# A ring of four places for streamed weights instead of six, with 15 instead of 17 streamed units

## The chip, the cores and the metric

The kernel runs on one core of a Trainium2 chip. The metric is the device time of one execution in microseconds, lower is better. Three runs of the kernel before took 1783.06, 1787.77 and 1794.25 us; the median is 1787.77 us. One more number is used throughout: the profiled execution, whose rows are quoted, spans 1793.2 us from its first to its last instruction.

PE stands for TensorE, DVE for VectorE, ACT for ScalarE, POOL for GpSimd and SP for SyncE, which only issues transfers here. PEld is TensorE's weight load. A name with a q, such as SPq, is an engine's sequencer.

## The reference

```python
xn = layernorm(x)                          # x: 2048 tokens of 1024, bfloat16
out = x + A(xn) + B(xn)

def B(xn):                                 # w1: 1024 x 3584, w2: 3584 x 1024
    return gelu(xn @ w1 + b1) @ w2 + b2

def A(xn):                                 # 32 heads of 128; Wq, Wk, Wv: 1024 x 4096, Wo: 4096 x 1024
    mem = mem0                             # 8 rows of 1024
    for s in range(64):                    # segments of 32 tokens
        h = concat(mem, xn[32 * s: 32 * s + 32])       # 40 rows
        q, k, v = h @ Wq, h @ Wk, h @ Wv
        p = softmax(mask(q @ k.T / sqrt(128)))         # per head; memory columns are always seen
        o = (p @ v) @ Wo
        mem = o[:8]                        # carried into the next segment
        outs.append(o[8:])
    return concat(outs)
```

The memory rows that leave segment s enter segment s + 1, so the 64 segments run one after the other. Each of them multiplies 40 rows by all four weight matrices, 33.5 MB in bfloat16, which is more than the on-chip memory holds.

## The kernel before

**Two stages.** The first 440 us compute B for all tokens (with the layer norm), and keep x + B as rows in DRAM. The rest is the recurrence of A over 64 segments. In its products the 24 rows of a segment's first tokens and the 8 memory rows are the stationary operand (32 columns), and the weights stream past them as the moving operand. Four matmuls run side by side on four groups of 32 PE columns, so one product of 32 rows with a unit of weights is four matmuls of 128x512 (L830). The last 8 tokens of each segment, which nothing later depends on, are gathered over four segments into 32 "left" rows and multiplied once per group of four. Which left products fall into a segment makes four kinds of segment, `i4 = s % 4`: kind 0 has those of K1 and V0, kind 1 of Q0 and of O, kind 2 of Q1, kind 3 of K0 and V1.

**Units and passes.** The weights are 64 units of 128 partitions x 2048 values (512 KB, 4 KB in each partition). A segment goes through them in a fixed order: eight units each for the half passes K0, Q0, K1, Q1, V0, V1 and then sixteen for O. A unit is named by matrix, row and half; `Wc_K_3_0` is K's row block 3 in half 0. `half_pass` runs the first six groups, the loop over `O_UNITS` the last sixteen; `at` lists give what is done behind the n-th unit of a pass, such as the scores of heads (`scores`, L947 and L953), their sums (`sums`, L985 and L991), and `values` (L1039 and L1045).

**Resident and streamed units.** 47 of 64 units stay on chip during the recurrence (`RESIDENT`, each in a place named in `RES_PLACES`, which the first stage used before for other data). 17 are streamed: needed once per segment, fetched anew each time. `PLACED` has, for each kind of segment, one string per group of eight units, where an S stands for a streamed unit and a point for a resident one; inside a group of eight the order of the units is free, so the S's can be moved. `kind_order` turns it into the order of a segment.

Two of the 17 are not fetched from DRAM. `IN_PSUM`, the fourth streamed unit (in Q0), and `IN_BANKS`, the last one (in O), are kept in four PSUM banks and copied by DVE into the ring, two copies of 128x512 32-bit words each (`copy_bits`, L273). The other 15 come as one transfer each from contiguous copies `Wc_...` in DRAM, which the first stage made.

**The ring.** Streamed units pass through the places in `RING`. When the last product with a streamed unit is issued, `unit_done` calls `start_stream` with the place that comes free, and this starts the next streamed unit in the order `starts`: a transfer on SP's queue (L284) that waits for PE's last matmul on the old unit, or the DVE copies, which wait for the same. With six places a unit begins six streamed uses ahead of its own. `LATER` shifts the copied units back in that order, by four places, so their copy begins two streamed uses ahead and the units in between begin one use earlier. SP's queue has nothing but these transfers in the recurrence; the rows of the next segment, the residuals and the results go through POOL's queue (ACT's in the first seven segments), the small ones from a list, of which `unit_done` issues one or two per streamed unit.

**The end of a segment.** O's 16 products add into one PSUM bank; in kinds 0, 2 and 3 it is changed after nine units, so that ACT (L1106) and DVE (L1109) can fold the first half while PE goes on. O's first eight units read the outputs of heads 0 to 15 (`nat_home`), the last eight those of heads 16 to 31 (`outM`), of which ACT writes the first half and DVE the second (L1058). DVE adds the rest (L1224), PE transposes the memory rows (L320), DVE copies them beside the next segment's rows (L330), and the first K product can start. Meanwhile PE does some products of left rows ahead (`lead_products`). DVE also adds the residual (L1246).

Of the kernel before, what the change touches and what calls it, by code (L numbers as in the profile page):

```python
# [18 lines left out]
S = 2048  # L19
# [24 lines left out]


NUNIT = 64
STREAMED = 17
LOW = 3
SCRATCH = 320
SMALL = 3776  # L50
# [10 lines left out]
VALUES_0 = ((4, 4), (4, 4), (4, 4), (3, 5))  # L61
SUMS_1 = (6, 7, 6, 5)
VALUES_1 = (5, 5, 5, 5)
LATER = 4
LAG = 3
STREAM_BUFS = 6
WARM = 16
FILL = 7
BEGUN = 4
# [4 lines left out]
def pass_order():  # L74
# [12 lines left out]

ORDER = pass_order()
PLACED = (
    "..SS...." ".S..S..." "S....S.." "....S..S" "....S..." "S..S...S" "...S..S." "S....S.S",  # L90
    "...SS..." ".S..S..." "..S..S.." "....SS.." ".S......" "S..S...S" "...S..S." "S....S.S",
    ".SS....." "S...S..." "S....S.." "....S..S" "....S..." "S..S...S" "...S..S." "S....S.S",
    "..SS...." ".S..S..." "S.....S." "....S..S" "....S..." "...SS..S" "...S..S." "S....S.S",
)
IS_STREAMED = {unit: PLACED[0][n] == "S" for n, unit in enumerate(ORDER)}
assert all(placed.count("S") == STREAMED for placed in PLACED)

# [18 lines left out]
KEPT = (IN_PSUM, IN_BANKS)  # L116
assert len(RESIDENT) == NUNIT - STREAMED


@with_exitstack  # L120
def kernel(
# [65 lines left out]
    def slab(place):  # L187
        if place in low:
            return low[place]
        return slabs.tile([P, 2048], BF16, name="u", tag=place)  # L190
# [37 lines left out]


    NP1 = FC // 2  # L230
    RING = ["xn0", "xn1", "w1_0", "w1_1", "xn2", "xn3"]
    assert len(RING) == STREAM_BUFS
    EARLY = list(low) + ["spare0", "spare1"]
    RES_PLACES = EARLY + ["late2", "xt0", "xt1"] + [f"w1_{k}" for k in range(2, NP1)] + ["late0", "late1"]
    for k in range(7):
        RES_PLACES += [f"w2_{2 * k}", f"w2_{2 * k + 1}", f"gT{k}"]
    UNIT_AT = dict(zip(RES_PLACES, RESIDENT))
    UNIT_AT.update(zip(("xt2", "xt3"), RESIDENT[-2:]))
    LATE = RESIDENT[len(RES_PLACES):-2]
    res_tiles = {}  # L240
# [7 lines left out]
    def fetch(t, unit):  # L248
        w, i, u = unit
        if w == "O":  # L250
            h = 4 * i + 2 * u
            nc.sync.dma_start(out=t.rearrange("p (h d) -> p h d", d=DM), in_=Wo_v[:, h:h + 2, :])
        else:
            nc.sync.dma_start(out=t, in_=W_v[w][:, i, 2048 * u:2048 * u + 2048])

    def fetch_resident(*places):
        for place in places:
            unit = UNIT_AT[place]
            res_tiles[unit] = slab(place)[:, :]
            fetch(res_tiles[unit], unit)  # L260
# [3 lines left out]
    late_by = [  # L264
        LATER if unit == IN_BANKS or (unit == IN_PSUM and n >= STREAMED) else 0 for n, unit in enumerate(streams)
    ]
# [4 lines left out]
    def copy_bits(out, in_):  # L271

        nc.vector.tensor_single_scalar(out=out, in_=in_, scalar=0, op=ALU.bitwise_or)  # L273

    def start_stream(slot):
        if not starts:
            return
        n = starts.popleft()
        unit, t = streams[n], slab(slot)
        if unit in kept_in:  # L280
            for c0, bank in kept_in[unit]:
                copy_bits(t[:, c0:c0 + 1024].bitcast(U32), bank.bitcast(U32))
        elif unit in copies:
            nc.sync.dma_start(out=t[:, :], in_=copies[unit])  # L284
        else:
            fetch(t[:, :], unit)
        stream_tiles[n], slot_of[n] = t, slot
# [53 lines left out]
    def new_ps(way="ps"):  # L341
        k = turns[way][0]
        turns[way].rotate(-1)
        shape, kind = ([P, 512], F32) if way == "ps" else ([P, KT, P], BF16)
        ps = banks.tile(shape, kind, name=way, tag=f"bank{k}")
        place_of[id(ps)] = k, ps
        return ps

    with tc.tile_pool(name="ma", bufs=2) as ma:
# [235 lines left out]
        for tg in range(4):  # L585
# [18 lines left out]
            for fb in range(FC):  # L604
# [21 lines left out]
                if last and fb % 2:  # L626
                    place = f"w1_{fb // 2}"
                    if place in RING:
                        start_stream(place)
# [52 lines left out]
            else:  # L682


                start_stream("xn2")
                start_stream("xn3")
                pss = [new_ps() for _ in range(6)]
                pss += [banks.tile([P, 512], F32, name="ps", tag=f"bank{k}") for k in turns["pT"]]
                seg_banks = [place_of[id(ps)][0] for ps in pss[:6]] + list(turns["pT"])
# [627 lines left out]
```

## Time and profile before

| what | before |
|---|---|
| median of three runs | 1787.77 us (1783.06 to 1794.25) |
| span of the profiled execution | 1793.2 us |
| granted clock of TensorE, mean | 0.997 |
| mean time from one segment's end (L320) to the next, 62 of them | 21.40 us |
| the same by the kind of the segment that ends, 0 / 1 / 2 / 3 | 21.5 / 22.6 / 20.3 / 21.3 us |
| units transferred per segment, bytes | 15 x 512 KB |
| all bytes moved by DMA | 594.46 MB |
| PE, DVE, ACT busy in the recurrence (440 to 1767 us) | 1249, 714, 514 us |

The span runs from the first to the last instruction; what lies around it is not shown, and the span lies between the median and the longest of the three runs. Busy time of PE is the union of its matmuls' shown lengths, and a 128x512 matmul is shown with 379 ns although the next group of four starts 215 ns after it, so PE counts as busy for a little while after it has nothing to do. A row such as "PE acc L1088 <- DMA u<-Wc_O" in the view of waits means: PE sat idle ahead of a matmul of line 1088 until a transfer into a place of the ring landed, that of a unit of O. The DMA share is the mean busy share of 16 DMA engines; where transfers overlap on an engine it can pass 1.

### The profile page before, as it was taken

To read this page: it belongs to the slowest core of one execution; us is meant where nothing else is said; L and a number is where in the kernel's file an instruction comes from. 1 tells how busy PE (TensorE), PEld (TensorE's weight loads), DVE (VectorE), ACT (ScalarE), POOL (GpSimd) and SP (SyncE) were. 2 spreads that over 40 slices of the span, in tenths; PEclk is the share of its full clock that TensorE was granted. 3 is DMA by queue.
4 is the path that set the end of the run, shared out by engine and by line. 5 is a ranking of instruction groups with operands and counts; after the bars stand their busy time and mean duration, and the time that the engine had idled before them with its cause. 6 is when DMAs were issued, how large, how long until landed. Compare 5 with 4: busy or idle time off the path is not lost.

```text
span 1793.2 us, 71764 instructions
## 1 busy us (share of the span) xinstructions
PE 1699.9 (95%) x31164; PEld 889.9 (50%) x31164; DVE 986.1 (55%) x2642; ACT 687.1 (38%) x1756; POOL 299.3 (17%) x586
## 2 busy tenths in 40 slices
PE   9999999998999999999999999999999999999998
PEld 5444444444554545555555555555545554444544
DVE  7657383835555555555555555555555455555554
ACT  6334160703333433333343333333334343333333
POOL 0000001401221111212121111112111111111211
PEclk9999999999999999999999999999999999999999
DMA  9455222879999999999999999999999999999998
GB/s 263 158 163 170 71 64 51 270 261 351 391 391 377 396 385 389 387 385 378 388 394 368 385 380 379 383 399 386 366 392 386 362 390 383 375 372 378 381 392 317
DMA packets 232832, 594.46 MB, mean 332 GB/s; under 512 B 57715, under 2 KB 88035, under 8 KB 232516
## 3 DMA queue, kind: packets, MB, share of 16 engines
q1 hardware_dynamic: 197584, 567.08, 84.4%
q0 software_dynamic: 16896, 16.85, 2.9%
q10 hardware_dynamic: 18036, 5.94, 1.3%
q8 instruction: 244, 4.00, 0.9%
q14 instruction: 72, 0.59, 0.1%
HBM read 573.43 MB, written 28.90 MB: 336 GB/s over the span
## 4 chain that ended last, share of the span: by engine, by line
PE 73%; DMA 16%; issue 3%; DVE 3%; ACT 2%; ACTq 1%; SPq 1%; DVEq 0%; POOL 0%; POOLq 0%
PE acc L830 37%; PE acc L1088 12%; PE ps L534 10%; DMA u<-Wc_O 10%; PE ps L662 6%; DMA u<-Wc_V 4%; PE ps L693 3%; PE acc L1039 1%; ACT mixed L999 1%; ACTq L459 1%; PE mixed L947 1%; DMA u<-Wc_Q 1%; DVE pd_main L1012 1%; SPq L521 1%; PE mixed L953 1%
## 5 line engine op out<-in xcount | busy, mean ns | idle before, releaser
L830 PE MATMUL acc<-u,hr_home 128*32 128x512 bf16 x11520 | 757.9, 380 | 15.7 <-issue 5.5
L830 PEld LDWEIGHTS <-hr_home 128*32 128x32 bf16 x12288 | 338.5, 96 | 291.1 <-issue 37.7
L830 PE MATMUL acc<-u,hrL 128*32 128x512 bf16 x2880 | 252.5, 380 | 4.0 <-issue 1.4
L534 PE MATMUL ps<-u 128*128 128x512 bf16 (+1 forms) x992 | 195.0, 358 | 0.0
L273 DVE TENSOR_SCALAR u<-kept 128x512 uint32<-128x512 uint32 x254 | 163.3, 685 | 55.2 <-PE acc L830 38.0
L1088 PE MATMUL acc<-u,d_oL 128*32 128x512 bf16 x2592 | 170.3, 381 | 15.0 <-DMA u<-Wc_O 8.0
L882 ACT CAST d_oL<-acc 128x512 bf16<-128x512 f32 x143 | 82.0, 585 | 263.2 <-PE acc L830 247.8
L1088 PE MATMUL acc<-u,kq 128*32 128x256 bf16 (+1 forms) x2884 | 138.3, 314 | 16.9 <-DMA u<-Wc_O 12.8
L662 PE MATMUL ps<-u 128*128 128x512 bf16 x672 | 147.1, 381 | 0.0
L1088 PEld LDWEIGHTS <-kq 128*32 128x32 bf16 x3908 | 106.0, 98 | 81.0 <-issue 27.3
L534 PEld LDWEIGHTS <-u 128*128 128x128 bf16 x992 | 91.7, 98 | 101.5
L1012 DVE TENSOR_TENSOR pd_main<-kq,mixed 128x320 bf16<-128x320 bf16 x128 | 62.5, 488 | 130.5 <-ACT mixed L999 129.6
L909 ACT CAST kq<-acc 128x256 bf16<-128x256 f32 x256 | 89.0, 375 | 115.9 <-PE acc L830 84.4
L913 DVE STREAM_TRANSPOSE kq<-kq 128x256 bf16<-128x256 bf16 x256 | 98.2, 422 | 49.6 <-ACT kq L909 49.6
L1279 POOL DMA_DIRECT2D out_dram<-hr_home x168 | 85.1, 514 | 221.4 <-DVE hr_home L1246 221.4
L886 ACT CAST kq<-acc 128x512 bf16<-128x512 f32 x128 | 75.2, 587 | 105.5 <-PE mixed L953 105.5
L830 PEld LDWEIGHTS <-hrL 128*32 128x32 bf16 x3072 | 86.2, 97 | 58.8 <-issue 6.2
L977 DVE TENSOR_TENSOR kq<-kq,mixed 128x96 bf16<-128x96 bf16 (+1 forms) x256 | 38.1, 190 | 130.7 <-ACT kq L967 75.9
L662 PEld LDWEIGHTS <-u 128*128 128x128 bf16 x672 | 65.9, 98 | 79.6 <-issue 1.4
L611 ACT ACTIVATE u<-ps,b1col 128x512 bf16<-128x512 f32 x112 | 76.4, 683 | 66.5 <-PE ps L534 63.6
L1088 PEld LDWEIGHTS <-d_oL 128*32 128x32 bf16 x2592 | 65.0, 96 | 71.0 <-issue 25.1
L999 ACT ACTIVATE mixed<-mixed,small_consts 128x160 f32<-128x160 f32 x256 | 94.3, 368 | 8.6
(126 smaller groups left out, 1926.2 us busy)
## 6 DMA issues: line engine op xcount, KB each, us to landing
u<-Wc_K SPq DMA_DIRECT2D x256, 512.0 KB
u<-Wc_V SPq DMA_DIRECT2D x256, 512.0 KB
u<-Wc_O SPq DMA_DIRECT2D x256, 512.0 KB
u<-Wc_Q SPq DMA_DIRECT2D x192, 512.0 KB
u<-in_B_w_dram SPq DMA_DIRECT2D x28, 512.0 KB
u<-in_A_Wq_dram SPq DMA_DIRECT2D x13, 512.0 KB
u<-in_A_Wv_dram SPq DMA_DIRECT2D x12, 512.0 KB
u<-in_A_Wk_dram SPq DMA_DIRECT2D x9, 512.0 KB
```

The source lines that it names most:

```text
L273: nc.vector.tensor_single_scalar(out=out, in_=in_, scalar=0, op=ALU.bitwise_or)
L534: nc.tensor.matmul(ps[:, SEG * s0:SEG * s1].rearrange("p (s t) -> p s t", t=SEG), lhsT=w1_sb[fb // 2][:, kt, (fb % 2) * P:(fb % 2 + 1) * P ...
L611: nc.scalar.activation(out=xb[:, :], in_=ps[:, :], func=ACT.Identity, bias=b1col[:, fb:fb + 1], scale=1.0)
L662: nc.tensor.matmul(ps[:, :], lhsT=gts[fc // 4][:, fc % 4, t * P:(t + 1) * P], rhs=w2_sb[fc // 2][:, fc % 2, cs], start=(fc == 0), stop=(fc ...
L830: nc.tensor.matmul(o, lhsT=lhs[:, i, :], rhs=m, start=(i == seq[0]), stop=(i == seq[-1]), tile_position=(0, 32 * j),)
L882: cp(out=out, in_=ps.rearrange("p (h e) -> p h e", e=32))
L909: nc.scalar.copy(out=q_home[:, h0:h1, NL:40], in_=ps[:, 32 * h0:32 * h1].rearrange("p (h e) -> p h e", e=32))
L913: nc.vector.transpose(out=half, in_=half)
L999: nc.scalar.activation(out=mixed[:, 160 * b:160 * b + 160], in_=mixed[:, 0:160], func=ACT.Exp, scale=-1.0, bias=off[:, b:b + 1],)
L1012: nc.vector.tensor_tensor(out=pdA.rearrange("p c b q -> p b c q"), in0=prA[:, None, :, :].to_broadcast([P, 2, 4, 40]), in1=dd, op=ALU.mult,)
L1088: nc.tensor.matmul(acc[r0:r0 + rows, 0:256 * len(blocks)], lhsT=lhsT, skip_group_check=True, rhs=o_columns(t, k, blocks), start=start, sto ...
L1279: loads.dma_start(out=out_flat[rows, 256 * j:256 * j + 256], in_=res[32 * j:32 * j + NX, :])
```

## The change

The ring has four places (`RING` without xn2 and xn3), and the two places taken from it hold resident units, so 49 units are resident and 15 streamed. Two of the 15 are still kept in PSUM, so 13 are transferred per segment. `LATER` is 1: a copied unit begins three streamed uses ahead of its own use, the unit behind it five, all others four. The S's in `PLACED` stand at other points in each kind of segment; where in the first stage two streams were started into xn2 and xn3, two resident units are fetched. With other units streamed, the names behind some places change; PE's products are the same.

```diff
-STREAMED = 17
+STREAMED = 15
...
-LATER = 4
+LATER = 1
 LAG = 3
-STREAM_BUFS = 6
+STREAM_BUFS = 4
...
 PLACED = (
-    "..SS...." ".S..S..." "S....S.." "....S..S" "....S..." "S..S...S" "...S..S." "S....S.S",
-    "...SS..." ".S..S..." "..S..S.." "....SS.." ".S......" "S..S...S" "...S..S." "S....S.S",
-    ".SS....." "S...S..." "S....S.." "....S..S" "....S..." "S..S...S" "...S..S." "S....S.S",
-    "..SS...." ".S..S..." "S.....S." "....S..S" "....S..." "...SS..S" "...S..S." "S....S.S",
+    "..SS...." ".S...S.." "......S." "...S...S" "....S..." "S..S...." "S...S..." "S.....SS",
+    "..S..S.." "..S.S..." "..S....." ".S...S.." ".......S" "....S..S" "....S.S." ".S..SS..",
+    "SS......" "S...S..." "S......." "SS......" "..S....." "S..S...." "S....S.." ".S....SS",
+    "..S.S..." ".S..S..." "S......." "....S..S" "......S." "..S.S..." "S..S...." "S....S.S",
 )
...
-    RING = ["xn0", "xn1", "w1_0", "w1_1", "xn2", "xn3"]
+    RING = ["xn0", "xn1", "w1_0", "w1_1"]
...
-    RES_PLACES = EARLY + ["late2", "xt0", "xt1"] + [f"w1_{k}" for k in range(2, NP1)] + ["late0", "late1"]
+    RES_PLACES = EARLY + ["late2", "xt0", "xt1"] + [f"w1_{k}" for k in range(2, NP1)] + ["late0", "late1", "xn2", "xn3"]
...
-                start_stream("xn2")
-                start_stream("xn3")
+                fetch_resident("xn2")
+                fetch_resident("xn3")
```

## The prediction

> **What bounds the kernel now.** I read the page first, then the busy time by stage, then PE's waits, and last the rows around the end of one segment. From the page:
>
> ```profile
> PE 1699.9 (95%) x31164; PEld 889.9 (50%) x31164; DVE 986.1 (55%) x2642; ACT 687.1 (38%) x1756; POOL 299.3 (17%) x586
> ...
> DMA  9455222879999999999999999999999999999998
> ...
> q1 hardware_dynamic: 197584, 567.08, 84.4%
> ```
>
> By stage (columns: window, length, busy time and instructions of PE, PEld, DVE, ACT and POOL, clock, DMA share, GB/s):
>
> ```profile
> 320.00:440.00 120.00, 115.19 (x1012) 53.91 (x1010) 66.98 (x158) 40.30 (x76) 27.62 (x51) 1.00 0.85 298
> 440.00:1767.00 1327.00, 1249.38 (x28156) 678.09 (x28148) 713.79 (x1964) 513.51 (x1455) 249.87 (x471) 1.00 1.00 383
> ```
>
> The recurrence is 1327 of 1793 us, 62 segments of 21.40 us on average, and in it the DMA engines are busy all the time (share 1.00) while PE is busy 94%. One streamed unit (0.524 MB) costs q1's 84.4% x 1793.2 us over 567.08 MB, so 1.40 us; 15 transferred per segment make 21.0 us. So the transfers and PE are both at their limit, and PE shows it little:
>
> ```profile
> PE acc L1088 <- DMA u<-Wc_O: 20.8, 45, 1.5
> ...
> PE acc L830 <- DMA u<-Wc_V: 4.3, 8, 1.3
> ...
> PE acc L830 <- DMA u<-Wc_Q: 2.0, 2, 1.1
> ```
>
> That is 27 us of idle PE. The idle time is too small by what a matmul's shown length (379 ns) hides: a unit of four matmuls follows the next in 0.215 us (five units in the 1.26 us of the x20 row below, whose last matmul is 0.38 us long). Measured from start to start against that pace, 120 matmuls of the recurrence that begin 42 ns after a landing begin 50 us late in all: **0.8 us per segment**. The end of a segment, where later one price is read:
>
> ```profile
> 906.18 1.23 PE L1088 MATMUL acc<-u,kq 128*32 128x256 bf16 x32
> 907.23 0.83 PE L830 MATMUL acc<-low,hrL 128*32 128x512 bf16 x12
> ...
> 908.80 0.60 PE L830 MATMUL acc<-low,hr_home 128*32 128x512 bf16 x8
> ...
> 910.54 1.26 PE L830 MATMUL acc<-u,hr_home 128*32 128x512 bf16 x20
> ```
>
> From the end of the last O product (907.41) to the first K product of the next segment (908.80) are 1.39 us, in which PE does some of the left rows' products ahead.
>
> **What goes: throughput.** Two of 15 transfers per segment go (64 x 2 = 128 of 960 issues at L284); PE's work and the two PSUM copies (2 x 682 ns on DVE each) stay. The transfers need 13 x 1.40 = 18.2 us of a segment, 85%. The 50 us in which PE waits for a saturated queue go, if nothing takes their place.
>
> **What comes: latency.** A place is refilled when its unit is done, four streamed uses ahead instead of six (five for the unit after a copied one). I call the time from the freeing unit's end to the start of the use, with PE not held up, the margin. In the order of the placements, n-th streamed unit by (n-4)-th, with 0.215 us per unit, 0.43 for an O unit of kind 1 (left rows too), 1.39 for the segment's end and some 0.2 to 0.5 for the scores between Q0 and Q1 (L947 and L953 run from 913.99 to 914.6):
> - second K unit: freed by the O unit at place 56 (57 for kinds 2 and 3). Kind 0: 10 units + 1.39 = 3.54; kind 1: 12 units, 3.97; kind 2: 6 x 0.43 + 1 unit, 4.19; kind 3: 10 units, 3.54.
> - first Q unit: freed by the next O unit. Kinds 0, 1, 3: 11 units + 1.39 = 3.75; kind 2: 3 x 0.43 + 8 units, 4.4.
> - Q1's second unit: freed by Q0's first. 21, 18, 16, 21 units and the scores: 5.0, 4.2, 3.6, 4.7.
> - the others 4.35 to 6.6.
>
> Against it stands the time of one transfer. The trace records 16 landing marks of each (no view prints them for SP's queue); the last counts. In the saturated recurrence it comes 6.6 us after the issue (median). A transfer that finds nearly empty queues there (30 cases, the one before landed within 3.3 us) takes 3.7 to 6.4, mean 4.9. In the stage before, fetches issued one by one every 3.45 us (14 cases, 340 to 401 us) take 3.4 to 4.7, mean 3.9. With 85% load and at most four in flight I take **4.7**, near the first.
>
> By the Trainium skill ("DMA: Bandwidth & Descriptors", "Anatomy of one DMA") a transfer takes about 2.0 us plus its bytes at 436 GB/s, an estimate of 3.2 us here. By that every margin would do, which is the second rival below; of the 44 rows none is this fast.
>
> At 4.7 PE waits per segment (a wait for one unit lengthens the margin of those freed before it): kind 0 1.16; kind 1 0.73 + 0.22 + 0.5; kind 2 0.51 + 1.1; kind 3 1.16. The sum is 5.38, on average 1.34, times 63 is 85 us; units with margins of 4.35 to 4.6 add some 5. So **90 us come and 50 go: +40**.
>
> **Instruction fetch.** 68 times in the recurrence PE begins 0.15 to 1.7 us late with no wait, always at a multiple of 256 instructions and 1.2 to 1.7 us after a 16 KB packet of q8 landed: 47 us. The packet starts later the more transfers are outstanding (2.4 us after the boundary below 1.5 of them, 3.4 above 3), and below 1.5 the mean delay is 0.10 us per fetch against 0.21 over all 221. With the shorter queue I take two thirds, -16 us; bounds -47 and, if blocks that follow each other faster bring all to the slowest group's 0.37 us (2.5 to 3 outstanding), +35.
> The Trainium skill ("Runtime: NRT & Kernel Launch", "Instruction fetch mechanics") has this cost mostly hidden; the trace disagrees, with the 47 us. By the page this term would be 0 and the sum 16 us higher.
>
> **The copies.** Three uses ahead instead of two. The Q0 unit's copy now stands right behind L1246 on DVE and waits for the first K unit; behind it queue L896's transpose and the q copies, which wait for ACT's L882 at the end of the K pass anyway. The last O unit's copy (1.29 us, the 904.47 row of L273) moves ahead of L1058's DVE half in kinds 0, 2 and 3 and makes it up to 0.7 us late. That half is heads 8 to 15 of the second group, first read at O place 60, some 0.86 us after place 56: covered, 0; read at place 56 it would cost up to 0.7 x 48 = 34 us. On SP the transfers behind a waiting one wait for places that come free later still: 0. Two fetches into xn2 and xn3 replace two stream starts at the same point of SP's queue: 0. Two fewer DRAM copies ahead of the recurrence, where the share is 0.41: 0. The list of small POOL stores is served 15 instead of 17 times per segment, and nothing waits on it: 0.
>
> **Sum.** -50 + 90 - 16 = **+24 us**. The profiled execution spans 1793.2 us, 5.4 over the median of the three runs; on the median this is 1787.8 + 24 = 1812.
>
> **The rivals.** All differ in the landing time, which decides steeply: per 0.3 us some 40 us.
> - *The lighter queue answers faster, 4.0 us* (the rows of 340 to 401 us, at DMA shares of 0.66 to 0.68). Waits: 0.46, 0.03 + 0.22, 0.4 and 0.46, mean 0.39, 25 us in all. -50 + 25 - 16 = -41: **1747**. It decides below some 4.45. The Trainium skill speaks for it ("DMA: Bandwidth & Descriptors", "Latency and other measured facts": lighter HBM load, smaller fixed cost); against it, packets of 4 KB took 184 ns on average at 326 to 360 us, at low load, and 169 in the saturated recurrence. Chance 0.15.
> - *No margin is short* (3.5 us or less): -50 - 16 = -66: **1722**; the fastest of the 44 rows took 3.4 us, most of them over 3.7. By the rule of "Anatomy of one DMA" in the Trainium skill this is what happens. Chance 0.03.
> - *4.4 us, loss and gain cancel*: 0.86, 0.43 + 0.22 + 0.2, 0.21 + 0.8, 0.86, mean 0.9, 56 us; -50 + 56 - 16 = -10: **1778**. Chance 0.25.
> - *Forecast, 4.55 to 4.85*: 1793 to 1832 by the same sums. Chance 0.41.
> - *The queue stays as slow as lone transfers are now, 5.0 us*: 1.46 + 0, 1.03 + 0.22 + 0.8, 0.81 + 1.4, 1.46 + 0.3, and 1.0 in the four kinds together for further units with margins below 5: 2.1 per segment, 134 us; -50 + 134 - 16 = +68: **1856**. Chance 0.16.
>
> That the change does not do what it says (a transfer of a unit still queued behind another's place) would show as 15 issues per segment; SP's program has 13.
>
> The range is **1760 to 1862**: it leaves out half of the 4.0 us case and the 1722 below, and less than half of the slowest above, 0.18 in all. A measurement of this kernel tells some 1% from no change, 1769.9 to 1805.6; faster 0.18, within 0.27, slower 0.55.
>
> **What would show it.** Right: the DMA share of the recurrence falls to 0.85 to 0.9; PE's waits on Wc_O at L1088 all but vanish and those on Wc_K and Wc_Q at L830 take their place, most on the second K unit and Q1's second; last landings at 4.5 to 5 us; PE late at fetch boundaries by 20 to 40 us. Wrong on the fast side if few waits on DMA are left. Wrong in its steps if L1088 waits for L1058's DVE half, or if waits spread evenly over all units.

## The result: slower by 7.6%, and the profile after

| what | before | after |
|---|---|---|
| median time | 1786.94 us (1783.06 to 1794.25, 4 runs) | 1924.49 us (1912.37 to 1925.76, 4 runs) |
| ratio to before, 95% interval | | 1.0755 (1.0715 to 1.0794) |
| span of the profiled execution | 1793.2 us | 1924.0 us |
| PE late behind a landing, start to start, in the recurrence | 50.4 us, 120 matmuls | 210.3 us, 265 matmuls |
| PE late at instruction fetch | 46.9 us, 68 boundaries | 5.4 us, 11 boundaries |
| last landing of a streamed unit after its issue, median | 6.6 us | 5.44 us (shortest 3.42) |

The forecast was 1812 us with a range of 1760 to 1862. The direction was right, the size was not.

The page of the kernel after, sections 1 to 4 (busy time, slices, the queue of the streamed units, the chain that ended last):

```profile
PE 1720.7 (89%) x31164; PEld 891.6 (46%) x31164; DVE 981.3 (51%) x2642; ACT 687.9 (36%) x1756; POOL 299.0 (16%) x586
...
DMA  9373315789989888888988888989988988888887
...
q1 hardware_dynamic: 179152, 499.96, 75.9%
...
PE 47%; DMA 43%; ACT 3%; issue 2%; DVE 2%; ACTq 1%; SPq 1%; DVEq 0%; POOL 0%; POOLq 0%
```

The transfers are no longer busy all the time (8 and 9 where there were only nines), 12% fewer bytes pass q1, and yet PE's share of the span fell to 89% and 43% of the chain consists of waits for transfers. I read this as a queue of which too little is asked at a time; the experiments below test it. In the recurrence (window, length, busy time and instructions of PE, PEld, DVE, ACT and POOL, clock, DMA share, GB/s):

```profile
445.00:1765.00 1320.00, 1154.36 (x25674) 619.39 (x25667) 647.69 (x1795) 468.63 (x1325) 228.64 (x431) 1.00 0.89 306
```

The DMA share is 0.89, as the prediction's 0.85 to 0.9 has it. PE's waits in the kernel after (total us, times, longest):

```profile
PE acc L830 <- DMA u<-Wc_Q: 95.0, 86, 3.0
PE acc L830 <- DMA u<-Wc_K: 23.6, 36, 1.7
PE acc L830 <- DMA u<-Wc_V: 20.1, 33, 1.6
PE acc L1088 <- DMA u<-Wc_O: 19.9, 32, 1.4
```

158.6 us of idle PE stand here where there were 27. The waits on Wc_O at L1088, which should have all but vanished, are as long as before; the new ones are on Q, K and V. The shown length of a matmul hides part of each wait again: start to start the lateness is 210.3 us. By unit (sums over the recurrence, from the landing marks and PE's starts): the first Q unit (Q_1_0) 71.0, Q1's second (Q_7_1) 43.4, the second K unit (K_3_0) 30.3, the O units 30.7, V1's second (V_3_1) 18.0, the other five 13.7 (without the last segment).

One end of a segment in the kernel after, first PE's rows and then those of SP's queue (start, length, what, idle time before and its releaser):

```profile
910.67 1.05 PE L1088 MATMUL acc<-u,kq 128*32 128x256 bf16 x32
911.54 1.04 PE L830 MATMUL acc<-u,hrL 128*32 128x512 bf16 x16
912.51 0.21 PE L320 MATMUL mixed<-ident_mem,kq 128*128 128x32 bf16 x2
...
914.81 1.26 PE L830 MATMUL acc<-u,hr_home 128*32 128x512 bf16 x20 [0.46 <-DMA u<-Wc_K]
916.67 0.40 PE L830 MATMUL acc<-u,hr_home 128*32 128x512 bf16 x4 [0.60 <-DMA u<-Wc_Q]
```

```profile
910.23 0.32 SPq L284 DMA_DIRECT2D u<-Wc_K  x1
911.54 0.32 SPq L284 DMA_DIRECT2D u<-Wc_Q  x1
911.96 0.37 SPq L284 DMA_DIRECT2D u<-Wc_K  x1
```

K_3_0 is issued at 910.23; its last mark comes at 914.77, 4.54 us later, and PE starts on it at 914.81. Q_1_0 is issued 1.31 us behind it, at 911.54, and lands at 916.63, **5.09 us** after its own issue: when it was issued, K_3_0 still had 3.2 us to go on the same queue. PE has waited 0.64 us for the first (start to start), which gave the second 0.64 us more, and must still wait 0.79 us for the second.

### The profile page after: what moved, and what is told of

The parts are those of the page before. It is cut to its first block, busy times and chain, and to the rows that moved or that the text cites. A ratio compares the mean times of both kernels' runs of the same rounds, so it can differ in the third digit from the quotient of the medians.

```text
span 1924.0 us, 71535 instructions
## 1 busy us (share of the span) xinstructions
PE 1720.7 (89%) x31164; PEld 891.6 (46%) x31164; DVE 981.3 (51%) x2642; ACT 687.9 (36%) x1756; POOL 299.0 (16%) x586
## 3 DMA queue, kind: packets, MB, share of 16 engines
q1 hardware_dynamic: 179152, 499.96, 75.9%
## 4 chain that ended last, share of the span: by engine, by line
PE 47%; DMA 43%; ACT 3%; issue 2%; DVE 2%; ACTq 1%; SPq 1%; DVEq 0%; POOL 0%; POOLq 0%
DMA u<-Wc_Q 21%; PE acc L830 19%; PE ps L534 10%; DMA u<-Wc_V 9%; DMA u<-Wc_O 9%; PE acc L1088 8%; PE ps L662 6%; DMA u<-Wc_K 4%; PE ps L693 3%; ACT mixed L999 1%; ACTq L459 1%; PE acc L1039 1%; DVE pd_main L1012 1%; SPq L521 1%; ACT mixed L996 1%
## 5 line engine op out<-in xcount | busy, mean ns | idle before, releaser
L830 PE MATMUL acc<-u,hr_home 128*32 128x512 bf16 x11520 | 785.3, 383 | 146.9 <-DMA u<-Wc_Q 95.0
L830 PEld LDWEIGHTS <-hr_home 128*32 128x32 bf16 x12288 | 348.6, 97 | 454.2 <-issue 200.3
L1088 PE MATMUL acc<-u,d_oL 128*32 128x512 bf16 x2592 | 165.7, 381 | 4.5 <-DMA u<-Wc_O 4.0
L1088 PE MATMUL acc<-u,kq 128*32 128x256 bf16 (+1 forms) x2884 | 132.5, 311 | 17.6 <-DMA u<-Wc_O 15.9
L1088 PEld LDWEIGHTS <-kq 128*32 128x32 bf16 x3908 | 102.6, 96 | 80.0 <-ACT kq L1058 24.4
L1185 POOL DMA_DIRECT2D hr_home<-res_d x57 | 31.7, 556 | 386.1 <-PE acc L1088 239.6
```

The source lines that it names most:

```text
L830: nc.tensor.matmul(o, lhsT=lhs[:, i, :], rhs=m, start=(i == seq[0]), stop=(i == seq[-1]), tile_position=(0, 32 * j),)
L1088: nc.tensor.matmul(acc[r0:r0 + rows, 0:256 * len(blocks)], lhsT=lhsT, skip_group_check=True, rhs=o_columns(t, k, blocks), start=start, sto ...
```

## The experiments

All times are medians; ratios are to the kernel before on the same chip. The first six columns are settings and time, the last two PE's lateness in the recurrence behind landings and at instruction fetch, start to start, from each run's profiled execution.

| run | streamed | places | LATER | time, us | ratio (95% interval) | landings, us | fetch, us |
|---|---|---|---|---|---|---|---|
| before | 17 | 6 | 4 | 1786.94 | | 50.4 | 46.9 |
| after | 15 | 4 | 1 | 1924.49 | 1.0755 (1.0715 to 1.0794) | 210.3 | 5.4 |
| six_places | 15 | 6 | 3 | 1755.13 | 0.9799 (0.977 to 0.9829) | 0.4 | 39.7 |
| five_places | 15 | 5 | 2 | 1771.8 | 0.9892 (0.9858 to 0.9926) | 30.4 | 31.3 |
| half_bytes | 15, halved | 4 | 1 | 1720.5 | 0.9608 (0.958 to 0.9636) | 5.2 | 0.0 |
| half_K | 15, one halved | 4 | 1 | 1843.39 | 1.0296 (1.0258 to 1.0334) | 131.1 | 5.9 |
| old_points | 15 | 4 | 1 | 1936.3 | 1.082 (1.0763 to 1.0876) | 230.0 | 6.0 |
| later_2 | 15 | 4 | 2 | 1878.04 | 1.0505 (1.045 to 1.0561) | 122.8 | 5.7 |
| spread_points | 15 | 4 | 2 | 1862.12 | 1.0419 (1.0351 to 1.0487) | 130.2 | 14.6 |
| sixteen_in_five | 16 | 5 | 2 | 1804.4 | 1.0083 (1.0051 to 1.0114) | 79.7 | 20.6 |
| seventeen_in_four | 17 | 4 | 2 | 2053.83 | 1.1499 (1.1421 to 1.1577) | 345.3 | 0.2 |

### More places, all else kept

```diff
-LATER = 1
+LATER = 3
-STREAM_BUFS = 4
+STREAM_BUFS = 6
...
-    RING = ["xn0", "xn1", "w1_0", "w1_1"]
+    RING = ["xn0", "xn1", "w1_0", "w1_1", "xn2", "xn3"]
...
+    SAME = {("V", 1, 0): ("V", 0, 0), ("V", 5, 0): ("V", 2, 0)}; OWN = [unit for unit in RESIDENT if unit not in SAME]; UNIT_AT = dict(zip(RES_PLACES, OWN))
...
-                fetch_resident("xn2")
-                fetch_resident("xn3")
+                start_stream("xn2")
+                start_stream("xn3")
```

`SAME` names two resident units whose products read another unit's place. LATER 3 with six places, or 2 with five, lets the copies begin three streamed uses ahead, as in the kernel after.

> The kernel after (15 streamed units, its points, copies begun three streamed uses ahead) with a ring of six places. Two resident units of V are not fetched and their products read the place of another unit of V, which frees the two places; only this part of the result is left out, and PE has the same products. Theory (the depth of the ring is short: PE waits 210 us because a place is begun too few uses ahead of its use for a landing of 5.4 us): every unit gains about two uses, 2.8 us, so nearly all waits on landings go, at most 15 us stay, late starts at instruction fetch stay at 5 to 10 us, and the time is 1720 us (1705 to 1740). Rival 1 (the points of the streamed units, or the later copies, make PE wait): the points and the copies are unchanged, so the time stays at 1900 to 1930 us. Rival 2 (transfers are too slow at 13 per segment, whatever the depth): time above 1850 us and last landings that grow to 7 us or more.

Measured: 1755.13 us. With the same points, the same copies and the same number of transfers the waits on landings are gone: 0.4 us instead of 210.3. So with six places these points, these copies and 13 transfers per segment do not make PE wait; it waits when there are four. The time is 15 us above the expected range. In the view of waits one row of 0.2 us is left for a transfer into the ring, and several of the costlier rows are those without a releaser ("issue"):

```profile
PE acc L830 <- issue: 9.2, 17, 1.2
...
PE acc L1088 <- issue: 4.8, 10, 0.9
...
PE acc L1045 <- issue: 3.6, 3, 2.2
PE mixed L947 <- issue: 3.5, 4, 1.6
```

Start to start, 39.7 us of late starts stand at 55 of 222 boundaries of 256 instructions. I had expected 5 to 10 us of them, as in the kernel after. The last section comes back to this.

> As with six places, but five: one resident unit of V reads the place of another, and every unit begins one use, 0.9 to 1.7 us, earlier than in the kernel after. Theory (depth): the waits of 0.3 to 0.7 us on the second K unit and Q1's second go, those of 0.8 to 1.5 us on the first Q unit shrink to 0.3 or less, all waits on landings make 25 us (10 to 50), and the time is 1745 us (1720 to 1770). Rival 1 (points or copies): 1900 to 1930 us. Rival 2 (transfers too slow): above 1880 us.

Measured: 1771.8 us, 1.8 us above the expected range, with 30.4 us of waits on landings (25 expected) and 31.3 us at instruction fetch. The fifth place alone removes 180 of 210 us; the first Q unit now waits 3.7 us in all instead of 71.0, since it has 4.9 to 5.7 us from its issue to its use without a wait, where it had 3.8 to 4.4, and it lands at 4.3 to 4.9.

### Fewer bytes, same places

```diff
-            nc.sync.dma_start(out=t[:, :], in_=copies[unit])
+            cols = 1024 if part else 2048; nc.sync.dma_start(out=t[:, 0:cols], in_=copies[unit][:, 0:cols])
```

`part` holds for all transfers into a place behind its first (half_bytes), or only for K_3_0 (half_K); such a transfer writes over the tile that lies in the place.

> The kernel after, ring of four, but each transfer into the ring moves half the bytes: columns 0 to 1023 of the unit, packets of 2 KB; the other half of the place keeps old values, so that part of the result is left out, and PE has the same products. Theory (PE waits on a landing made of a fixed part and a part by bytes, queued behind the transfer ahead): the part by bytes is about 1.4 us of 5.4 when alone and more in a queue, so last landings fall to about 4.2 us (3.8 to 4.5), waits to 30 us (10 to 70), and the time is 1750 us (1725 to 1790). Rival (the landing is a fixed latency that bytes hardly change): landings stay above 5 us and the time above 1860 us. Rival (points or copies): the time stays above 1900 us.

Measured: 1720.5 us, 4.5 us below the expected range, and last landings with a median of 3.22 us after the issue, where I had 4.2. With that, four places are enough: 5.2 us of waits. Halving the bytes took 2.2 us off the landing, three times the 0.7 us that half a unit costs at 1.40 us each. I take the rest to be time behind other transfers, which are shorter too; no run measures that part alone. This is also the fastest that PE ran in any of the runs (it leaves half of the streamed values out), and no late start at instruction fetch is left in it. Its view of waits has no row without a releaser, and begins so:

```profile
PE acc L1039 <- DVE pd_main L1012: 8.0, 31, 0.3
PE acc L1039 <- ACT kq L882: 7.0, 15, 0.5
...
PE acc L830 <- DMA u<-Wc_Q: 2.0, 4, 1.0
```

> The kernel after, but the transfer of one unit per segment, the second streamed K unit (K_3_0), moves only columns 0 to 1023; that part of its values is left out. The first streamed Q unit is issued 1.3 us behind it. Theory (the Q unit lands 5.6 us after its issue because its packets queue behind those of K_3_0): K_3_0 lands 0.7 us earlier, its waits fall from 30 to about 5 us, the Q unit lands 0.7 us earlier but has 0.4 us less margin, its waits go from 71 to about 55 us; together 40 us less, 1885 us (1870 to 1900). Rival (the Q unit's landing time has nothing to do with the transfer ahead of it): it stays at 5.6 us, and the 0.4 us that the wait on K_3_0 lent it come back as its own wait, so the time stays at 1924 us (1912 to 1932).

Measured: 1843.39 us, 81 us less than after, twice what was expected and below the range. K_3_0 lands 3.6 us after its issue instead of 4.4, and its waits fall from 30.3 to 8.9 us. Q_1_0, whose own transfer is unchanged, lands 4.2 to 4.5 us after its issue instead of 5.3 to 5.7, and its waits fall from 71.0 to 24.7 us. So the Q unit lands late in large part because of the transfer ahead of it; 1.2 us earlier is more than the 0.7 us of transfer time that went, and that rest I can't explain. Q1's second unit, on which nothing was changed, waits 46.4 us (43.4 in after).

The row of Wc_Q in the view of waits, after and then half_K:

```profile
PE acc L830 <- DMA u<-Wc_Q: 95.0, 86, 3.0
```

```profile
PE acc L830 <- DMA u<-Wc_Q: 56.8, 72, 1.7
```

### The points and the copies

```diff
 PLACED = (
-    "..SS...." ".S...S.." "......S." "...S...S" "....S..." "S..S...." "S...S..." "S.....SS",
...
+    "..SS...." ".S..S..." "S......." "....S..S" "....S..." "S..S...." "...S..S." "S....S.S",
...
```

> The kernel after (ring of four, 15 streamed units, copies three uses ahead) with the points of the kernel before, less one S in the group of K1 and one in V1 of each kind. This undoes the new points alone. Going through the four kinds unit by unit with PE's start times of the run with half the bytes and, as landing times, the means of the run after grouped by how long the transfer ahead still had to go (4.0 us behind a free queue, 4.9 at 2.5 us to go, 5.3 at 3.7, 6.3 at 4.9), I estimate 163 us of waits for the kernel after (its trace shows 210) and 180 for this one. Theory (depth of the ring, not the points): about 20 us slower than after, 1941 us (1915 to 1965). Rival (the new points make PE wait): far faster than after, below 1850 us.

Measured: 1936.3 us, as expected; its interval overlaps that of after, so the points of the kernel before, less two, are no better than the new ones. The units that wait are others, while the sum is about the same (230.0 us, 210.3 in after): the second and third largest are now V_3_1 with 46.8 us and K_3_0 with 29.1, behind Q_1_0 with 67.3.

```diff
-LATER = 1
+LATER = 2
```

> The kernel after with LATER 2: a copied unit begins two streamed uses ahead, as in the kernel before, and two units behind each copy begin five uses ahead instead of one. This undoes the earlier copies alone. By the same estimate waits fall from 163 to 147 us. Theory (depth): 1905 us (1885 to 1920). Rival 1 (copies begun three uses ahead, which hold a place for longer and stand elsewhere in DVE's order, are the main loss): below 1860 us. Rival 2 (two uses ahead is too late for a copy, two of 682 ns each, when uses stand close): above 1930 us.

Measured: 1878.04 us, 46 us less than after, more than the 19 us expected and below the range. A copy that begins one use later leaves its place one use longer to a transfer, and two units behind each copy instead of one have five uses ahead. The second K unit now waits 6.6 us (30.3) and Q_1_0 22.2 (71.0). Waits on landings fall by 87 us, but not all of that is gained, since the copy itself comes late in O:

```profile
PE acc L830 <- DMA u<-Wc_Q: 43.5, 57, 2.4
PE acc L1088 <- DVE u L273: 24.5, 16, 1.7
PE acc L1088 <- DMA u<-Wc_O: 23.0, 38, 1.5
```

The second row was not there in after. All 16 times are in segments of kind 2, 1.5 us each: there the last S's stand at places 57, 62 and 63 of the 64, so the copy for 63 is released when 57 is done, with five units of 0.215 us left for its 2 x 683 ns. But that is not when it starts. In the segment shown here the product at place 57 ends at 940.95 us, and DVE does the fold of the first nine O units (L1109) ahead of the copy:

```profile
941.56 0.85 DVE L1109 TENSOR_TENSOR d_oL<-acc,d_oL 64x256 f32<-64x256 f32 x2 [1.18 <-ACT d_oL L1106]
942.44 1.29 DVE L273 TENSOR_SCALAR u<-kept 128x512 uint32<-128x512 uint32 x2
```

```profile
943.78 0.40 PE L1088 MATMUL acc<-u,kq 128*32 128x256 bf16 x8 [1.14 <-DVE u L273]
```

The copy starts 1.5 us after its place is free. The program puts the fold ahead of the product at place 57, so a copy released at 57 stands behind it in DVE's order and one released at 56, as in kinds 0 and 3, ahead of it. Both rivals hold a part: a copy begun early costs a place, one begun late, and here behind the fold, is not ready. A choice for each of the two copies, or an S at 56 in kind 2, was not run.

```diff
-LATER = 1
+LATER = 2
 PLACED = (
...
+    ".S..S..." "...S..S." "....S..." ".S.....S" "...S...." "S..S...." "..S...S." "S...S..S",
+    "S.....S." ".....SS." "...S...." "S......S" "......S." "..S....S" "..S....S" ".S...S.S",
+    "S..S...." "...SS..." "..S....." "S....S.." ".....S.." "S....S.." "...S..S." "..S...SS",
+    ".S..S..." "..S..S.." ".S......" "S......S" "......S." "..S..S.." ".S...S.." "S..S...S",
 )
```

> LATER 2 and other points for the 15 streamed units, ring of four: spread so that no use follows four others closely, found by trying many with the same estimate, which gives 127 us of waits instead of 163. Theory (with four places no choice of points makes the time from a place's release to the next use longer than landings everywhere: four uses are 5.6 us of a segment of 21 us on average, landings 4.5 to 5.5): 1880 us (1855 to 1900), still slower than before. Rival (the points alone are at fault, and a ring of four is deep enough with better ones): 1805 us or less.

Measured: 1862.12 us, within the expected range. Points that spread the uses give 16 us more than later_2 had (the intervals overlap), 62 in all on the kernel after, and stay 4% above the kernel before. The waits are spread too: no unit but Q_7_1 (33.0 us) has over 18 us. Four uses last 5.4 us on average where PE doesn't wait (4/15 of the 20.2 us that a segment takes in half_bytes), and the landings of this run have a median of 5.52 us, so with four places the mean time between release and use is no longer than a landing, and some uses come late.

### Half of the change, and the depth alone

```diff
-STREAMED = 15
+STREAMED = 16
-LATER = 1
+LATER = 2
-STREAM_BUFS = 4
+STREAM_BUFS = 5
...
-    RING = ["xn0", "xn1", "w1_0", "w1_1"]
+    RING = ["xn0", "xn1", "w1_0", "w1_1", "xn2"]
...
-                fetch_resident("xn2")
+                start_stream("xn2")
```

> Half of the change, complete in its result: 16 streamed units, a ring of five, 48 resident, LATER 2, points spread by the same estimate. It gives 73 us of waits, where it gives 60 for the kernel before (whose trace shows 50), and late starts at instruction fetch should be between the 31 us of five places and the 47 of before. Theory: 1800 us (1780 to 1820), no gain on the kernel before. Rival (one transfer less per segment, 1.4 us of a bound of 21.0, is worth more than a place of the ring): 1765 us or less.

Measured: 1804.4 us, 0.8% above the kernel before, as expected: 79.7 us of waits (73 estimated) and 20.6 us at fetch. None of the kernels run here that compute all values beats the kernel before.

```diff
-LATER = 4
+LATER = 2
-STREAM_BUFS = 6
+STREAM_BUFS = 4
...
-    RING = ["xn0", "xn1", "w1_0", "w1_1", "xn2", "xn3"]
+    RING = ["xn0", "xn1", "w1_0", "w1_1"]
...
-                start_stream("xn2")
-                start_stream("xn3")
```

> The depth alone: the kernel before with its 17 streamed units and its points, a ring of four instead of six (the two places stay unused), LATER 2 so that copies begin two uses ahead as there. Together with the kernel before (17 in six), after (15 in four) and the run of 15 in six places it completes a square. By the estimate of the other runs (60 us of waits for the kernel before, 163 for after, where the traces show 50 and 210) it has 319 us of waits, late starts at instruction fetch some 40 us fewer than before. Theory (depth): 2030 us (1980 to 2110), so the two streamed units fewer are worth some 100 us in a ring of four and 35 in a ring of six. Rival (the loss came with the two units made resident or the new points, not with the places): 1800 us or less. Rival (transfers and depth cost the same bytes over and over: 15 transfers at 1.40 us bound a segment whatever the ring): below 1860 us.

Measured: 2053.83 us, within the expected range. This completes the square:

| | six places | four places |
|---|---|---|
| 17 streamed units | 1787 us | 2054 us |
| 15 streamed units | 1755 us | 1924 us |

Two streamed units fewer are worth 32 us in a ring of six and 130 in a ring of four. Two places fewer cost 169 us with 15 units and 267 with 17. The change pays 169 for 32. (Within a row the points and the copies are the same. Between the rows the points differ, 12 us by old_points, and copies begin two uses ahead above and three below, 46 us by later_2.) The residents behind it bear no blame: they are the same in six_places but for the two units not fetched.

## Why the prediction was right in its direction and wrong in its size

**The steps that held.** The bound was read rightly: with the queue no longer saturated the 50 us on a full queue go (0.4 us at 15 units in six places), and the loss comes from places that are filled too late. The margins were right to 0.3 us. From the freeing unit's end to the use, with the waits taken out, the trace of after has for K_3_0 3.6, 4.0, 4.2 and 3.8 us by kind (3.54, 3.97, 4.19 and 3.54 in the prediction), for Q_1_0 3.8, 3.8, 4.4 and 4.0 (3.75, and 4.4 in kind 2), for Q_7_1 5.2, 4.3, 3.7 and 4.8 (5.0, 4.2, 3.6 and 4.7). K_3_0 and Q_7_1 wait, as named, though the first Q unit, which was not named, waits more than either; L1088 waits nowhere for L1058's DVE half, but its waits on Wc_O, which were to vanish, stayed (19.9 us of 20.8). DMA share and the number of transfers were right.

**The step that failed** is "with 85% load and at most four in flight I take 4.7": one landing time for all. It was worked out from transfers that found the queue nearly empty, and applied to transfers that don't. The rows of 340 to 401 us of the kernel before already held the others: the fetches issued there at 379.75, 386.66 and 393.57 us land after 3.9, 4.0 and 4.1 us, and those issued 0.38 us behind each of them after 4.7, 4.9 and 5.0; the prediction took only the 14 "issued one by one". Sorted by how long the transfer ahead still had to go at the issue, the landings of after are (663 issues from 450 to 1650 us, nine above 6 us left out):

| transfer ahead has to go, us | under 1.6 | 1.6 to 2.2 | 2.2 to 2.8 | 2.8 to 3.4 | 3.4 to 4.0 | 4.0 to 4.6 | 4.6 to 5.2 | 5.2 to 6.0 |
|---|---|---|---|---|---|---|---|---|
| cases | 6 | 47 | 70 | 132 | 149 | 121 | 87 | 42 |
| last landing after the issue, us | 4.0 | 4.7 | 4.9 | 5.2 | 5.3 | 5.7 | 6.3 | 6.9 |

4.7 us is the value for a queue that is almost free, which 53 of these issues meet. K_3_0 lands even earlier (4.2 to 4.6): its 56 us of the predicted sum (mean 0.89 per segment) became 30.3. Q_1_0 is issued right behind K_3_0 at the end of O and lands at 5.3 to 5.7, so that what K_3_0's wait lent it, 0.5 us on average, did not cover it, and my 3.5 us (0.22 in one kind of four) became **71.0**. This one unit is more than half of the 120 us by which 90 became 210. Q_7_1 was given 25 us and took 43.4. The other ten units, of which only those with "margins of 4.35 to 4.6" had a price, 5 us in the sum, took 65 us: their margins are 4.5 to 6.6 us, and they land at 4.9 to 6.8 us on average by unit and kind, with a standard deviation of 0.3 to 0.7 us within a column of the table. The queueing was shown by half_K: with half of K_3_0's bytes gone the Q unit landed 1.2 us earlier.

The transfer ahead is not the whole of it. Q_1_0 finds 3.1 us to go on average, for which the table has 5.2 us, and lands at 5.6; K_3_0 finds 2.4, for which it has 4.9, and lands at 4.5. Packets of other queues don't explain it: they take the least time while Q_1_0 is under way (0.18 us of the 16 engines' time, 0.20 to 0.36 for the other units). The transfer behind may: the next one is issued 0.5 us behind Q_1_0 and 1.4 us behind K_3_0, and among all landings of after with 2.5 to 3.5 us to go ahead of them, those with the next issue within 1 us take 5.4 us (62 cases), those with it 1.4 us or more behind 4.9 (110). No run separates this, and it stays open.

**Instruction fetch** was taken at -16 us within -47 to +35, and measured -42 (46.9 to 5.4). The reason given, a lighter queue, is not the main one: at equal numbers of transfers outstanding a fetch costs far less in after than in six_places, which has the same transfers and late starts of 39.7 us. Where PE waits for landings anyway, I read, the next instructions arrive meanwhile; that is argued, not shown, and the last section has the numbers.

**The sum** with the measured terms: landings +160 (50.4 to 210.3), fetch -42, waits on ACT and DVE +5, late starts with no wait outside fetch +3, starts late by under 40 ns each +4; together +130, and the spans differ by 130.8.

**The rivals.** "The lighter queue answers faster, 4.0 us" and "4.4 us" fell: 4.0 is the landing behind a free queue. "No margin is short" fell too: the shortest of some 810 landings took 3.42 us, and the table has 4.0 for a free queue. (The Trainium skill, "DMA: Bandwidth & Descriptors", "Anatomy of one DMA", gives its two terms for transfers that GpSimd issues. The units are issued by SP, so the prediction's estimate of 3.2 us carried the rule over to another path; every landing of after was longer than the estimate, and no run here tests the rule on its own path.) Nearest came the slowest rival, 5.0 us and 1856. I priced one landing time against the margins and never asked at which time the transfer ahead is issued, although the same list of margins shows K_3_0 and Q_1_0 freed by two O units that end 1.3 us apart. By the slope "per 0.3 us some 40 us" the 134 us at 5.0 come to 210 at some 5.6, near the measured median of 5.44, but that is luck: at one landing time of 5.6 for all K_3_0 alone would wait some 110 us, and it waited 30.3.

## What to carry to other kernels

Places of a ring are worth bytes in flight: with transfers that land 5 to 6 us after their issue and four uses in 5.4 us, taking two of six places cost 169 us where the two transfers saved were worth 32. When a refill's margin is compared with its landing, take the landing behind the transfer that is issued just ahead of it, not that of a lone one, and look for two places that come free together. And a queue busy 0.89 of the time with an engine that waits for it is no contradiction: look at how many transfers are under way as well as at the share.

## What the runs showed of the hardware

**Where PE waits for landings, it waits less for instructions.** Late starts at boundaries of 256 instructions make 46.9 us before, 39.7 in six_places, 31.3 in five_places, 20.6 in sixteen_in_five, 5.4 in after, 0.2 in seventeen_in_four: from six_places on, the more PE waits for landings (0, 30, 80, 210, 345 us), the less it waits for instructions (before, with 50 us of waits, has the fullest queue). The order is not strict: later_2, half_K and spread_points wait 123 to 131 us for landings and 5.7, 5.9 and 14.6 us for instructions. With 2.5 to 3 transfers outstanding when a 16 KB packet starts (a transfer counted by the share of its 16 marks still to come), a fetch makes PE some 0.22 us late on average in six_places (49 fetches) and 0.04 in after (48). So some 35 us of what a removed wait seems to be worth can be taken back: six_places and half_bytes both have next to no waits on landings, and the 35 us between their times are about the 39.7 us of fetch that half_bytes lacks. There the 16 KB packets start some 0.9 us behind a boundary, in six_places some 2.2 to 3.1 us: fewer bytes in the queue remove late starts too, without a wait that covers them.

**A less busy queue takes longer per byte.** q1's share of the span, which is the time that its packets took, over its bytes gives 1.40 us per unit of 512 KB before and 1.53 after (75.9% x 1924.0 us / 499.96 MB x 0.524 MB), 1.47 with six places. Taking two transfers of 15 away took 12% of the bytes and 3.5% of the queue's time (84.4% x 1793.2 = 1513 us, 1460 after).
